# Input loads sent out in turns behind the squares of the feed-forward, and a reordered head, in a fused sparse-attention and feed-forward kernel

## The chip, the cores and the metric

The kernel runs on one NeuronCore of a Trainium2 chip. The metric is the device time of one execution, in microseconds (us); the lower, the better. The engines are TensorE (PE; its weight loads are shown as PEld), VectorE (DVE), ScalarE (ACT), GpSimd (POOL) and SyncE (SP). Each works through its own queue in order, and semaphores tie them together. POOL and SP also issue transfers (DMAs).

## What is computed

Batch 8, 8 heads, 576 tokens, head size 64; model width 512, hidden width 2048.

```python
scores = scale * np.matmul(q, k.transpose(0, 1, 3, 2))
rel = pos[:, None] - pos[None, :]
mask_local   = (rel >= 0) & (rel < 32)
mask_strided = (rel >= 0) & (pos[None, :] % 32 == pos[:, None] % 32)
# heads 0-3 use mask_local, heads 4-7 mask_strided
attn = softmax(where(mask, scores, -1e9))
x = (attn @ v) as [batch * 576, 512]           # 4608 tokens
h = x @ w_in                                   # 512 -> 2048
g = s * relu(h)**2 + b
out = g @ w_out                                # 2048 -> 512
```

Inputs and outputs are fp32; on the chip the kernel works in fp16 and sums in fp32. The loads that POOL issues convert from fp32 to fp16 on the way.

## The kernel before

**Attention.** A batch is cut into four pairs of heads, m = 0 and 1 local, m = 2 and 3 strided (`pair_steps`). The local heads are cut into 6 bands of 96 queries, so that a band needs 128 keys: its own 96 and the 32 before; `rows_before` copies those 32 rows of v to the partitions ahead. The strided heads are cut into residue groups of 72 tokens. For each pair, q and k have to be brought with the head size onto the partitions. In early batches PE does that (transposes at L429 and L437); in later ones a DMA transpose on SP does: `k_dma` (L480: local from batch `KB_DMA` = 4, strided from 3) and `q_dma` (L502: local from `QB_DMA` = 6, strided from `QS_DMA` = 3), after which `q_spread` copies q into a block-diagonal tile. PE then makes scores (L557), ACT takes the exponential (L575), DVE applies the mask (L583), PE multiplies by v (L614), and DVE divides by the row sums (L629, L640). The result x is transposed into `xT` by PE (L662) or by DMA; strided pairs of batches 4 to 6 take the way over `x_dram`, a store and a transposing load (`x_out`, `x_in`; `XS_DMA` = 4).

**Feed-forward.** It runs over 9 blocks T of 512 tokens. First product: 16 tiles of 128 hidden units, each of four 128x128x512 matmuls (L907). ACT takes the relu (L934) and DVE or ACT squares two tiles at a time into `gT` (L944, L942). One such pair of tiles is a pair of squares. Second product: L965 for blocks 0 to 2; from block 3 on L875, a seven-product form. `keep_running` (L1201) puts matmuls without use into the first microseconds, where PE has no data yet.

**Loads.** `load_qk`, `load_vl` and `load_vs` issue a batch's loads on POOL: local q and k (`ql`, `kl`, in four pieces of one head each where they go to a DMA transpose), strided q and k (`qs`, `ks`), v of the local heads (`v_loc`, the bands) and v of the strided heads (`v_str`, in early batches over `vs`). In `fetch_qk` a one-element copy into `gate` on POOL (L1036) waits for the transposes of the batch before, and then the whole batch is issued at once. Batch 0's v of local heads comes by SP into `vl_stage`, as fp32, in four loads, and POOL casts it. w_in comes in three pieces (512, 512 and 1024 columns), w_out in four. `second` issues batch 1 and w_out after batch 0 and w_in.

**Order.** The order on all engines is fixed when the kernel is built, by a planner (`Plan`). It keeps an estimated clock `plan.t` along PE's work. A `Step` is a piece of PE work with its needs; a post is work for another engine, given out by `flush` once its needs are met on the estimated clock, to the engine that would end first. `LAT` is what is added to an engine's end before its result counts as there ("D", "X" and "Y" stand for SP's transposes, stores of x and loads of x); `landing` does the same for loads. PE takes attention steps while they lag behind their due share (`due`), feed-forward steps otherwise. Only the order comes out of this: on the chip semaphores decide when each instruction starts.

Of the kernel before, what the change touches and what calls it, by code (L numbers as in the profile page):

```python
# [9 lines left out]
FP16 = mybir.dt.float16  # L10
# [5 lines left out]
class Plan:  # L16
# [7 lines left out]
    LAT = {"A": 70.0, "V": 70.0, "P": 70.0, "D": 12000.0, "X": 7000.0, "Y": 12000.0}  # L24
# [4 lines left out]
    def __init__(self):  # L29
        self.t = 0.0  # L30
        self.done = {}
        self.pend = []
        self.free = {"A": 0.0, "V": 0.0, "P": 7000.0, "D": 0.0, "X": 0.0, "Y": 0.0}
        self.banks = {}
# [82 lines left out]
class Step:  # L117
    def __init__(self, fn, ns, needs=(), group=None, keys=(), posts=(), after=None):
        self.fn, self.ns, self.needs, self.group = fn, ns, needs, group
        self.keys, self.posts, self.after = keys, posts, after  # L120
# [3 lines left out]
def kernel(  # L124
# [11 lines left out]
    nc = tc.nc  # L136
# [20 lines left out]
    for p in range(SQ):  # L157
        for c in range(SQ):
# [30 lines left out]
               for i, n in enumerate((512, 512, 1024))]  # L189
# [21 lines left out]
    def x_free(b):  # L211
# [22 lines left out]
    vl_stage = w_out_sb.rearrange("p f m -> p (f m)").bitcast(FP32)[:, 0:NL].rearrange(  # L234
        "p (h t d) -> p h t d", h=4, d=D)
# [34 lines left out]
    for tl in p_bufs[False]:  # L270
        nc.vector.memset(tl[:, 16 * SQ:], 0.0)

# [40 lines left out]
    def load_vl(b):  # L313
        vl = v_loc[b % NV]
        for h in range(4):
            nc.gpsimd.dma_start(out=vl[LPAD:128, h, :, 0:D], in_=v_band(b, h))  # L316
# [8 lines left out]
    def load_w_in():  # L325
        wv = moe_w_in.rearrange("(c p) f -> p c f", p=128)
        for i, at in enumerate((0, 512, 1024)):
            nc.gpsimd.dma_start(out=w_in_sb[i], in_=wv[:, :, at:at + w_in_sb[i].shape[2]])
# [26 lines left out]
    def cast_v(b, loc, mm, key):  # L355
        nt, np_, dst = (LT, 128, v_loc) if loc else (ST, SQ, v_str)

        def g(eng):
            src = vl_stage if loc else loaded[b, "vs"].rearrange(
                "p (h t d) -> p h t d", h=4, d=D)  # L360
            for h in range(2 * mm, 2 * mm + 2):
                copy_on(eng, out=dst[b % NV][0:np_, h, :, 0:D], in_=src[:, h])
        n = nt * D
        plan.post([key], {"P": 1000.0} if loc else {"A": 2 * (170 + 0.83 * n), "V": 540.0,
                                                           **({"P": 1500.0} if b == 0 else {})}, g,
                  [("cast", b, mm) if loc else ("in", "vs", b, mm)])
        if loc:
            rows_before(b, mm, ("cast", b, mm))

    def rows_before(b, mm, key):  # L370

        hs = slice(2 * mm, 2 * mm + 2)
        vl = v_loc[b % NV]
        src = vl_stage[:, :, :, 0:D] if b == 0 else vl[:, :, :, 0:D]

        def g(eng):
            copy_on(eng, out=vl[0:LPAD, hs, 1:LT, 0:D], in_=src[128 - LPAD:128, hs, 0:LT - 1])
        plan.post([key], {"P": 800.0} if b == 0 else {"A": 700.0, "V": 350.0}, g, [("in", "vl", b, mm)])
# [30 lines left out]
    def pair_steps(b, m):  # L409
# [10 lines left out]
        def trans(name, j, group):  # L420
            alone = loc and b < HEAD_T

            def f():
                if j == 0:
                    st["p" + name] = bank(group).bitcast(FP16)[:, 0:S]
                if alone:
                    for e in range(2):
# [12 lines left out]
            s = Step(f, 70 if alone else 35, needs=[("in", name + sfx, b, mm)],  # L440
                     group=group if j == 0 else None)
            if j == nt - 1:
# [35 lines left out]
        x_by_dma = b >= 2 if loc else XS_DMA <= b < B - 1  # L478
# [418 lines left out]
    def ff1(T, ft, ct, group, cts=(0, 1, 2, 3), early=False):  # L897
        tok0 = T * PS
        def f():
            if ft == 0 and ct == cts[0]:  # L900
                gts[T] = gp.tile([128, NFT, PS], FP16, tag="gT", name="gT")
            if ct == cts[0]:
                gts["h", T, ft] = bank(group)
            at = tok0 % (NX * S)
            n = min(PS, NX * S - at)
            for lo, hi in ((0, n), (n, PS))[:1 + (n < PS)]:
                nc.tensor.matmul(  # L907
                    out=gts["h", T, ft][:, lo:hi],
                    lhsT=w_in_sb[min(ft // 4, 2)][:, ct].rearrange(
                        "p (c x l) -> p c l x", x=128, l=4)[:, max(ft // 4 - 2, 0), ft % 4],  # L910
                    rhs=xT[ct][:, (at + lo) % (NX * S):(at + lo) % (NX * S) + hi - lo],
                    start=(ct == cts[0] and lo == 0), stop=(ct == cts[-1] and hi == PS))
# [109 lines left out]
    def landing(cost):  # L1022

        nonlocal ring
        ring = max(ring, plan.t + 2000.0) + cost

        return ring + (6000.0 if plan.t > 60000.0 else 600.0)
# [4 lines left out]
    def fetch_qk(b):  # L1032
# [6 lines left out]
        for name in ("q", "k"):  # L1039
            if b >= (QB_DMA if name == "q" else KB_DMA):  # L1040
                arrive(both(name + "l", b), landing(4600))
                continue
            if b < HEAD_T:
                arrive(both(name + "l", b), landing(1500))
                continue
            plan.done["raw", name, b] = landing(1700 if b > 1 else 1450)
            for mm in range(2):
                pair_post(b, name, mm, ("raw", name, b))
        for name in ("qs", "ks"):
            arrive(both(name, b), landing(2000 if b > 1 else 1750))  # L1050
# [12 lines left out]
    def early_v(b):  # L1063
# [3 lines left out]
        plan.done["raw", "v", False, b] = landing(1800)  # L1067
# [3 lines left out]
    gate = const.tile([64, 4], FP16)  # L1071

    def after_landing(i, src):
# [3 lines left out]
    load_qk(0)  # L1077
    early_v(0)
    plan.free["P"] = 7100.0
    plan.free["V"] = 6500.0  # L1080
    AT = {"ql0": 5700.0, "kl0": 6800.0, "ql1": 7900.0, "kl1": 8900.0, "qs": 10100.0,
          "ks": 11600.0, "vs": 13600.0, "vl0": 7100.0, "vl1": 14700.0}
# [6 lines left out]
    stage_v(range(2, 4))  # L1089
# [3 lines left out]
    def weights_in(eng):  # L1093
# [4 lines left out]
        ring = 15300.0  # L1098
        for keys, cost in ([0], 2700), ([1], 2500), ([2, 3], 5000):
            arrive([("w_in", c) for c in keys], landing(cost))  # L1100

    for mm, at in (0, AT["vl0"]), (1, AT["vl1"]):
        plan.done["raw", "v", True, 0, mm] = at
        cast_v(0, True, mm, ("raw", "v", True, 0, mm))
# [7 lines left out]
    def second(eng):  # L1112
# [3 lines left out]
        plan.done["raw", "vl", 1] = landing(3200)  # L1116
# [5 lines left out]
    plan.post(both("vl", 0) + both("vs", 0) + [("w",)], {"P": 14000.0}, second, [("free",)])  # L1122
# [12 lines left out]
    for b in range(B):  # L1135
        for m in range(4):
            steps, last_av = pair_steps(b, m)
            att.append(steps)
            if b + 2 < B:

                if m == 0:
# [4 lines left out]
                        {"P": 2900.0 + (2200.0 if b + 2 >= QB_DMA else 0.0)},  # L1146
                        lambda eng, b=b: fetch_qk(b + 2), [("fetch", b + 2)])
                last_av.after = when_all("av", b, lambda b=b: plan.post(
                    [("fetch", b + 2)] + both("vs", b), {"P": 3600.0}, lambda eng: fetch_v(b + 2),
                    [("fetch_v", b + 2)]))  # L1150

    f1, f2 = [], []
    for T in range(NBLK):
# [26 lines left out]
        for ts in range(4):  # L1180

            parts = 2 if T == NBLK - 1 and ts == 3 else 1
            for part in range(parts):
                gr = Group("f2", F2B)
                for ft in range(NFT):
                    f2.append(ff2(T, ts, ft, gr, part, parts))
                    f2[-1].pos = T + 0.25 + (ts + (part + ft / NFT) / parts) / 4
    def keep_running(until):

        ghz = 1.2 if plan.t < 6000 else 2.4  # L1190
# [26 lines left out]
    while i2 < len(f2) or any(at_i[p] < len(att[p]) for p in range(len(att))):  # L1217
# [5 lines left out]
        active = [p for p in range(first, min(first + 4, len(att))) if at_i[p] < len(att[p])]  # L1223
        for p in active:
# [67 lines left out]
```

## Time and profile before

| | |
|---|---|
| time, median of 3 runs | 305.44 us (305.16 to 306.75) |
| the profiled execution: its time | 306.2 us |
| the profiled execution: its span, first to last instruction | 304.4 us |
| PE / PEld busy | 296.4 / 205.8 us |
| DVE / ACT / POOL busy | 216.6 / 183.9 / 99.3 us |
| granted PE clock | 1.00 throughout |
| read from HBM / written | 36.86 / 10.32 MB |
| packets of the DMAs | 100826, of them 80907 under 512 B |

The page cuts the span into 40 slices of 7.6 us; the mean busy share of the 16 DMA engines is at nine tenths or more in nearly all of the first 200 us, and PE is at 8 or 9 tenths throughout. In the profile's rows an entry such as `out<-in xcount` counts instructions with the same tiles; "[... <-X]" names what ended the idle time before a row. The duration of a matmul in the records [...]379 ns for 512 columns that start 216 ns apart. So counts are multiplied by the distance of starts here, and not by that mean. An issue time on POOL or SP is not the time of the transfer; a transfer's "us to landing" is given apart.

### The profile page before, as it was taken

What the parts mean: (1) busy time and instruction counts of PE and PEld (TensorE: products, weight loads), DVE (VectorE), ACT (ScalarE), POOL (GpSimd) and SP (SyncE); (2) the same over time, 40 slices, a digit from 0 to 9 for tenths busy, and PEclk for the clock granted to TensorE, in tenths of its full rate; (3) what the DMA queues carried; (4) which work ended last, traced back from release to release, by engine and by line L of the source; (5) the groups of instructions that cost most, each with busy time, mean ns of one, the idle gap of its engine ahead of it and who ended that gap; (6) DMA issues with size and microseconds to landing.
All of it is one profiled execution on the core that took longest, in us unless ns stands there. A gap on an engine that the chain in (4) does not pass through costs nothing.

```text
span 304.4 us, 6800 instructions
## 1 busy us (share of the span) xinstructions
PE 296.4 (97%) x2674; PEld 205.8 (68%) x2674; DVE 216.6 (71%) x474; ACT 183.9 (60%) x330; POOL 99.3 (33%) x146
## 2 busy tenths in 40 slices
PE   8998999999999999999999999999999999999995
PEld 3764655666555568767567776778888666766784
DVE  6665897698966688737997698777765366737563
ACT  2966963898747677478585946695725445445300
POOL 8771753930961095029502961200000000000000
PEclk9999999999999999999999999999999999999999
DMA  8999999999999699999999999944010200300123
GB/s 136 183 201 202 137 213 190 179 198 149 83 160 165 98 100 149 132 186 147 142 153 172 142 160 159 155 105 131 14 37 34 72 34 0 106 0 2 69 82 126
DMA packets 100826, 37.29 MB, mean 122 GB/s; under 512 B 80907, under 2 KB 97803, under 8 KB 100795
## 3 DMA queue, kind: packets, MB, share of 16 engines
q0 software_dynamic: 57232, 18.08, 60.1%
q1 hardware_dynamic: 43562, 18.78, 33.3%
q8 instruction: 21, 0.34, 0.5%
q14 instruction: 11, 0.08, 0.1%
HBM read 36.86 MB, written 10.32 MB: 155 GB/s over the span
## 4 chain that ended last, share of the span: by engine, by line
PE 83%; DMA 8%; DVE 3%; POOL 3%; issue 1%; ACT 1%; POOLq 0%
PE ps_f L907 36%; PE ps_f L875 20%; PE ps_f L965 12%; DMA kl<-in_k_dram 5%; PE ps_s L557 3%; PE ps_a L614 3%; DMA vs<-in_v_dram 2%; PE ps_s L875 2%; DMA xT<-x_dram 1%; PE ps_t L875 1%; PE ps_s L965 1%; PE ps_t L614 1%; PE ps_t L662 1%; PE ps_t L437 1%; PE ps_f L437 1%
## 5 line engine op out<-in xcount | busy, mean ns | idle before, releaser
L907 PE MATMUL ps_f<-xT,w_in_sb 128*128 128x512 f16 (+4 forms) x696 | 148.1, 340 | 0.0
L934 ACT ACTIVATE u<-ps_f 128x512 f16<-128x512 f32 x137 | 80.8, 595 | 72.6 <-PE ps_f L907 69.9
L907 PEld LDWEIGHTS <-w_in_sb 128*128 128x128 f16 x704 | 71.7, 113 | 33.1 <-DMA w_in_sb<-in_moe_w_in_dram 0.5
L875 PEld LDWEIGHTS <-gT 128*128 128x128 f16 x512 | 49.0, 98 | 12.5 <-issue 0.4
L965 PE MATMUL ps_f<-w_out_sb,gT 128*128 128x512 f16 x176 | 47.6, 379 | 0.0
L875 PE MATMUL ps_f<-w_out_sb,gT 128*128 128x256 f16 x312 | 44.2, 273 | 0.3 <-DVE o L806 0.3
L944 DVE TENSOR_TENSOR gT<-u 128x1024 f16<-128x1024 f16 x46 | 32.1, 697 | 15.1 <-ACT u L934 14.4
L942 ACT ACTIVATE gT<-u 128x1024 f16<-128x1024 f16 x26 | 27.5, 1057 | 0.7
L640 DVE TENSOR_TENSOR x_nat<-ps_a,rec 72x256 f16<-72x256 f32 (+1 forms) x55 | 25.3, 459 | 0.9
L316 POOL DMA_DIRECT2D v_loc<-in_v_dram x28 | 20.7, 759 | 14.3 <-DMA w_in_sb<-in_moe_w_in_dram 6.0
L965 PEld LDWEIGHTS <-gT 128*128 128x128 f16 x192 | 17.0, 98 | 11.1
L575 ACT ACTIVATE p_str<-ps_s 72x432 f16<-72x432 f32 (+1 forms) x45 | 20.1, 481 | 4.7 <-PE ps_s L557 4.6
L575 ACT ACTIVATE p_loc<-ps_s 128x384 f16<-128x384 f32 x46 | 20.8, 494 | 2.2 <-PE ps_s L557 1.8
L614 PEld LDWEIGHTS <-p_str 72*128 72x128 f16 x256 | 15.3, 98 | 7.3 <-issue 0.4
L747 DVE TENSOR_TENSOR gT<-gT 128x1024 f16<-128x1024 f16 x28 | 18.5, 683 | 1.4 <-ACT gT L942 1.3
L875 PE MATMUL ps_f<-w_mix,gT 128*128 128x256 f16 x144 | 19.3, 273 | 0.0
L875 PEld LDWEIGHTS <-S 128*128 128x128 f16 x160 | 15.5, 98 | 3.7
L629 DVE RECIPROCAL rec<-ps_a 72x4 f32<-72x4 f32 (+1 forms) x55 | 9.7, 177 | 11.2 <-PE ps_a L614 11.0
L321 POOL DMA_DIRECT2D v_str<-in_v_dram x16 | 13.0, 816 | 9.6 <-PE ps_f L907 5.6
L583 DVE TENSOR_TENSOR p_loc<-p_loc,masks 128x1152 f16<-128x1152 f16 x14 | 10.5, 750 | 7.6 <-ACT p_loc L575 7.4
L875 PE MATMUL ps_f<-w_mix,S 128*128 128x256 f16 x96 | 13.4, 273 | 0.0
L976 DVE SCALAR_TENSOR_TENSOR o<-ps_f,s_sb,bcs 128x512 f32<-128x512 f32 x11 | 8.2, 749 | 6.4 <-PE ps_f L965 6.2
(162 smaller groups left out, 413.2 us busy)
## 6 DMA issues: line engine op xcount, KB each, us to landing
out_dram<-o SPq DMA_DIRECT2D x34, 256.0 KB, 3.4
w_out_sb<-in_moe_w_out_dram POOLq DMA_DIRECT2D x4, 512.0 KB, 9.4
v_loc<-in_v_dram POOLq DMA_DIRECT2D x28, 72.0 KB, 8.5
qs<-in_q_dram POOLq DMA_DIRECT2D x6, 288.0 KB, 6.6
ks<-in_k_dram POOLq DMA_DIRECT2D x6, 288.0 KB, 8.0
ql<-in_q_dram POOLq DMA_DIRECT2D x5, 288.0 KB, 9.7
kl<-in_k_dram POOLq DMA_DIRECT2D x16, 72.0 KB, 3.8
v_str<-in_v_dram POOLq DMA_DIRECT2D x16, 72.0 KB, 9.9
```

Of the source, the lines that this page charges most:

```text
L316: nc.gpsimd.dma_start(out=vl[LPAD:128, h, :, 0:D], in_=v_band(b, h))
L321: nc.gpsimd.dma_start(out=vs[:, h, :, 0:D], in_=v[b, 4 + h].rearrange("(p j) d -> p j d", j=ST))
L575: nc.scalar.activation(out=st["pw", g][0:nk, 0:2 * n * nq], in_=st["s", g][0:nk, 0:2 * n * nq], func=AF.Exp, scale=scale)
L614: nc.tensor.matmul(out=st["a"][:, j % per, :], lhsT=st["pw", g][0:nk, i * nq:i * nq + WIDE], rhs=vt[0:nk, 2 * mm + e, j, :])
L640: nc.vector.tensor_tensor(out=st["x"][:, j0:j0 + per, 64 * e:64 * e + 64], in0=st["pa", e, j][0:nq, 0:per, 0:D], in1=st["rec", e, j][0:nq, ...
L747: nc.vector.tensor_tensor(out=at(out), in0=at(x), in1=at(y), op=op)
L875: nc.tensor.matmul(out=gts[name, T, t][:, 0] if halves else gts[name, T][:, t], lhsT=lhs(k, t), rhs=rhs(k), start=fresh and k == 0 and (ha ...
L907: nc.tensor.matmul(out=gts["h", T, ft][:, lo:hi], lhsT=w_in_sb[min(ft // 4, 2)][:, ct].rearrange("p (c x l) -> p c l x", x=128, l=4)[:, ma ...
L934: nc.scalar.activation(out=u, in_=gts["h", T, ft], func=AF.Relu)
L942: nc.scalar.activation(out=g, in_=u, func=AF.Square)
L944: nc.vector.tensor_tensor(out=g, in0=u, in1=u, op=ALU.mult)
L965: nc.tensor.matmul(out=gts[id_], lhsT=gts[T][:, ft, ts * 128:(ts + 1) * 128], rhs=w_out_sb[:, ft, cols], start=(ft == 0), stop=(ft == NFT ...
```

## The change

Seven things change together.

- **Turns.** From batch 4 (`SPREAD`) on, the loads of a batch are no longer issued at once. `spread_qk` and `spread_v` hand each load singly to `in_turn`. It groups them by `PER` = 3; the first of each group does a one-element copy from `gT` on POOL, which waits for a given pair of squares of the running block. The copies that wait for the transposes of k now stand ahead of the `ks` load only.
- **Planner.** `LAT` of D goes from 12000 to 7000 ns, of X from 7000 to 5500, of Y from 12000 to 5500; a queue "Z" without cost is added for posts that only hand out others. `landing` adds 4000 ns instead of 6000 after 60 us. Loads in turns count as landed 5000 ns after their issue.
- **Head, v of batch 0.** Only heads 0 and 1 come by SP through `vl_stage`; heads 2 and 3 come by one load on POOL, right into `v_loc`, ahead of `vs`.
- **v of batch 1** (the second band v) comes in one load rather than four.
- **w_in** comes in four pieces of 512 columns.
- **x of the last batch**: the strided pairs of batch 7 also take the way over `x_dram`.
- **Start.** The planner's clock starts at 1850 ns, the expected arrivals (`AT`) change, batch 0's transposes keep together once begun (`sticky`), and small parts of the `p_str` tiles are zeroed at the start.

```diff
-    LAT = {"A": 70.0, "V": 70.0, "P": 70.0, "D": 12000.0, "X": 7000.0, "Y": 12000.0}
+    LAT = {"A": 70.0, "V": 70.0, "P": 70.0, "D": 7000.0, "X": 5500.0, "Y": 5500.0, "Z": 0.0}
...
-               for i, n in enumerate((512, 512, 1024))]
+               for i, n in enumerate((512, 512, 512, 512))]
...
+        nc.vector.memset(tl[:, 0:12 * SQ].rearrange("p (g x) -> p g x", g=2)[:, 1, 0:56], 0.0)
+        nc.vector.memset(tl[:, 12 * SQ:12 * SQ + 56], 0.0)
...
     def load_vl(b):
         vl = v_loc[b % NV]
+        if b < 2:
+            nc.gpsimd.dma_start(
+                out=vl.rearrange("p h t d -> p (h t) d")[LPAD:128, :, 0:D],
+                in_=v.rearrange("b h (t p) d -> b p (h t) d", p=LQ)[b, :, 0:4 * LT])
+            return
...
-        x_by_dma = b >= 2 if loc else XS_DMA <= b < B - 1
+        x_by_dma = b >= 2 if loc else XS_DMA <= b
...
+    SPREAD, PER, LATE = 4, 3, 5000.0
+    turn = [0, 0]
+
+    def in_turn(fns, needs=()):
+
+        if turn[0] <= i1 // 8:
+            turn[0], turn[1] = i1 // 8 + 1, 0
+        for fn, keys in fns:
+            T, at = turn[0] // 8, turn[0] % 8
+            key = ("g", T, ff_order(T)[2 * at]) if T < NBLK else None
+
+            def go(eng, fn=fn, key=key, first=turn[1] == 0):
+                if first and key:
+                    nc.gpsimd.tensor_copy(out=gate[0:1, 0:1], in_=gts[key[1]][0:1, key[2], 0:1])
+                fn()
+            plan.post(list(needs) + [key] * (key is not None), {"P": 760.0}, go, keys, LATE)
+            turn[1] += 1
+            if turn[1] == PER:
+                turn[0], turn[1] = turn[0] + 1, 0
...
+            def load(name=name, src=src, ts=ts):
+                for mm in range(2) if name == "k" else ():
+                    if (b - 1, "kTs", mm) in loaded:
+                        nc.gpsimd.tensor_copy(out=gate[0:1, 2 + mm:3 + mm],
+                                              in_=loaded[b - 1, "kTs", mm][0:1, 0, 0:1])
+                if name == "q" and b == QS_DMA + 1:
+                    nc.gpsimd.memset(ts[64:SR], 0.0)
+                load_s(ts, src, b)
+            fns.append((load, both(name + "s", b)))
+        in_turn(fns)
...
+    nc.gpsimd.dma_start(
+        out=v_loc[0].rearrange("p h t d -> p (h t) d")[LPAD:128, 2 * LT:4 * LT, 0:D],
+        in_=v.rearrange("b h (t p) d -> b p (h t) d", p=LQ)[0, :, 2 * LT:4 * LT])
     early_v(0)
...
-    stage_v(range(2, 4))
...
-                        lambda eng, b=b: fetch_qk(b + 2), [("fetch", b + 2)])
+                        lambda eng, b=b: (spread_qk if b + 2 >= SPREAD else fetch_qk)(b + 2),
+                        [("fetch", b + 2)])
...
+    plan.t = 1850.0
...
+        active.sort(key=lambda p: not att[p][at_i[p]].sticky)
```

## The prediction

> **What bounds the kernel now.** I read the page's busy times first, then what TensorE (PE) waited for, then the order of its instructions at its longest waits, then POOL's queue.
>
> ```profile
> span 304.4 us, 6800 instructions
> PE 296.4 (97%) x2674; PEld 205.8 (68%) x2674; DVE 216.6 (71%) x474; ACT 183.9 (60%) x330; POOL 99.3 (33%) x146
> ```
>
> PE is busy for 97% of the span. The waits of PE say how much of the rest another engine could give back:
>
> ```profile
> PE ps_t L429 <- DMA ql<-in_q_dram: 1.4, 1, 1.4
> PE ps_s L1201 <- DVE w_mix L257: 1.1, 1, 1.1
> PE ps_t L429 <- DMA kl<-in_k_dram: 0.6, 1, 0.6
> PE ps_s L557 <- ACT kT_loc L338: 0.4, 1, 0.4
> PE ps_s L907 <- DMA w_in_sb<-in_moe_w_in_dram: 0.4, 1, 0.4
> PE ps_f L875 <- DVE o L806: 0.3, 1, 0.3
> PE ps_a L614 <- DVE x_nat L640: 0.2, 1, 0.2
> ```
>
> The columns are the total, the number of times and the longest, in us. Only the last two (0.5 us) fall after 33 us. From there on PE has work without a break until it ends at 301.2 us, and 3.2 us for the last output follow. So a gain can only come from the first 33 us or from less PE work; any new wait of PE after that is paid in full. In the head, PE's timeline:
>
> ```profile
> 23.00 4.05 PE L907 MATMUL ps_f<-xT,w_in_sb 128*128 128x512 f16 x18
> 28.49 0.45 PE L429 MATMUL ps_t<-ident,ql 96*64 96x96 f16 x12 [1.44 <-DMA ql<-in_q_dram]
> 28.77 0.42 PE L429 MATMUL ps_f<-ident,ql 96*64 96x96 f16 x12
> 29.12 1.49 PE L907 MATMUL ps_f<-xT,w_in_sb 128*128 128x512 f16 x6
> 31.23 0.45 PE L429 MATMUL ps_t<-ident,kl 96*64 96x96 f16 x12 [0.62 <-DMA kl<-in_k_dram]
> ```
>
> PE stands twice for batch 1: q lands at 28.5 us, k at 31.2. Whatever was lost or saved before 26.9 us is swallowed by the first of these waits. POOL's queue at the same time:
>
> ```profile
> 22.06 0.75 POOL L316 DMA_DIRECT2D v_loc<-in_v_dram  x1 [1.96 <-DMA w_in_sb<-in_moe_w_in_dram]
> 26.89 0.72 POOL L316 DMA_DIRECT2D v_loc<-in_v_dram  x1 [4.08 <-DMA w_in_sb<-in_moe_w_in_dram]
> 28.73 0.73 POOL L316 DMA_DIRECT2D v_loc<-in_v_dram  x1 [1.11 <-DMA ql<-in_q_dram]
> 31.47 0.72 POOL L316 DMA_DIRECT2D v_loc<-in_v_dram  x1 [2.01 <-DMA kl<-in_k_dram]
> ```
>
> Each load waits for the eighth load before it on this queue, so four v loads for batch 1 hold back all behind them. What the DMAs move falls from about 200 GB/s (17 to 30 us) to 51 at 32 us.
>
> [...]kT transposes land 2.9 us after issue (median), but qTl, issued at 150.8 and 180.5 us behind outstanding v loads, 8.6 to 9.3, and kT_alt at 119.9 us 9.9. [...]Dense runs of L907 here start 216 ns apart.
>
> **The change part by part.** The order of the built instructions, not only the diff, is used.
>
> Batch 7's strided x goes through DRAM: 16 PE transposes (80 to 64 of 72 columns) go. They start 32.5 ns apart in the trace (four in 0.13 us): **−0.5 us**. Added are two stores and two DMA transposes on SP. PE ends batch 7's attention some 16 us of its own work before the last block needs x; store, landing (3.4 as an output's), transpose (1.2) and its landing (2.7 to 4.8) make 8 to 10 and fit, and the DMA share there is below 0.25. With less room it could cost up to 2 us: kept for the range.
>
> Head. 32 matmuls of L907 still precede batch 1's q, but ten, not six, now precede its k: 4 × 0.216 = 0.86 us of work in place of a gap of 0.78 us (start to start, less the work): **−0.8**. The q wait itself: two of the four SP loads of batch 0's v (144 KB each) become one POOL load that writes half the bytes, 144 KB less ahead of q at about 200 GB/s: 0.7 us, between 0 (if packets, not bytes, count) and 1.0 (the dip at 13 to 16 us also goes): I take **−0.6**. w_in goes in four pieces: one POOL issue more (0.76), hidden because q lands after w_in anyway; the third piece is asked for only after q, at 29 us. One v load of batch 1 in place of four saves 3 × 0.73 us of POOL and lets w_out start some 2 us sooner; PE did not wait for w_out, so nothing. At worst its first head lands with the last, later by what three issues took (2.2 us), and PE asks for v 7 us after k: nothing. POOL loses a CAST of 1.2 us and two copies (1.16) ahead of q, DVE halves a memset of 1.34 and gains four small ones (about 0.06 each), PE's warm-up matmuls fall from 13 to 8 (0.43 us each, while it waits for the first q): all before 26.9 us, nothing. The planner's shorter latencies only change the order.
>
> Spread loads, batches 4 to 7. Before, batch 4's loads issue from 76.2 to 92.3 us and its scores start near 108. After, five or six gates copy one element of gT, then three loads follow each. In PE's order the first gate stands 20 us later, at 95.8 us of the old clock (its pair of squares ends 93.8; evicting and squaring take about 2). POOL issues 15 loads × 0.745 = 11.2 us, a memset of 1.8 and gates of some 2.5: again about 16 us. So the burst is hardly thinner, it is **later**. No PE work is saved. What becomes late is SP's transposes and q_spread. Behind a waiting gate stand POOL's other loads and no PE work directly; behind a late load on SP stand x and output transfers.
>
> The longest chain is strided k (load_s, then k_dma). From the first gate to the end of ks's issue I count 10.6 us for batch 4 (nine loads, memset, five gate copies with gaps of 0.45), 8.7 for 5, 11.3 for 6 (SP also has an x transpose of 1.3 ahead), 12.1 for 7. Then the load lands (288 KB rows: 5.2 to 8.3), SP issues (1.3), the transpose lands (2.9 quiet, 5.3 under loads as qT's). Sum: 20.0 to 25.5, 18.1 to 23.6, 22.0 to 27.5, 21.5 to 27.0. PE's own work from that gate to the first score that reads it: 20.6, 22.2, 23.4, 25.4. So the wait is 0 to 4.9, 0 to 1.4, 0 to 4.1, 0 to 1.6. Local q of batch 6 and 7 (qTl at 9 us) ends within 0.5 of its need. Since gates also hold later loads back, I take the low ends: **+0.2**, at most about 12.
>
> Sum: −0.5 − 0.8 − 0.6 + 0.2 = **−1.7 us**. The profiled execution took 306.2 us (span 304.4 and 1.8 around it), 0.8 above the median of 305.44. So 304.5 against that execution, and **303.7** against the median.
>
> **Rivals.** *Late k, slower*: the load and the transpose meet the same traffic as before, 8.3 and 5 us. For is that the burst keeps its 16 us and that transposes of 9 us occur amid loads; against, that the kT transposes all landed in 2.9 to 4.4. Priced at half of the upper waits (2.4 + 0.7 + 2 + 0.8 = 5.9) less the 1.9 gained: 309.4; at a quarter, 306.5. It decides for batch 4 from load plus transpose over 8.7 us (20.6 − 10.6 − 1.3); above 1.9 us over all batches it makes a loss. *Paid back, no change*: q of batch 1 lands at 28.5 as before and the chains cost 1 us: −1.3 + 1.0 gives 305.1. *The spread does nothing*: POOL is so far behind its gates that they never hold; then order and head alone count, 303.5; for it, issue time almost fills the gates' pace.
>
> **How the numbers follow.** A measurement of this kernel can tell about 0.5% (1.5 us) from no change: below 303.9 is faster, above 307.0 slower. Faster (head gain kept, chains in time, the third rival with it) 0.49; within 0.5% 0.26; slower by late k 0.25. The likeliest is 303.7. Its own range is 301.9 (q a further microsecond earlier, other head gaps gone) to 304.6 (the q wait kept). The range over the cases, 301.9 to 308.8, leaves out some 0.07 below and 0.13 above.
>
> **What would show it.** Right: PE's wait for kl gone and that for ql at or under 1.4 us; 64 transposes of x; no PE wait over 0.5 us on kT, kT_alt or qD; kT landing near 3 us. Wrong: PE (or its weight load) waiting at scores of batches 4 to 7 near 116, 146, 180 or 211 us, with kT landings over 4.5 us or ks over 6; or q of batch 1 landing later than 28.5.

## The result: an eighth slower, and the profile after

The changed kernel takes 347.81 us (median of 4 runs, 343.12 to 351.9); the kernel before, on the same chip, took 306.09 (305.16 to 306.75). The ratio is 1.125 (95% interval 1.116 to 1.135); it is taken from the two faster runs (343.12 and 345.58 us) alone, because the other two, the profiled one among them, lie over 1.5% above the fastest and ran at a lower granted clock (0.946 and 0.951 against 0.960). I had said 303.7, in a range of 301.9 to 308.8. The profiled execution is the longest of the four, so its waits are rather long. In the kernel of the first experiment below, profiled at 340.93 us, those for k and for `x_nat` stand again: kT_alt 9.2, kT_loc 4.7, kT 1.6 and x_nat 3.9 us.

The page of the changed kernel, busy times and granted clock (tenths of full speed in 40 slices of 8.75 us):

```profile
span 350.1 us, 6790 instructions
PE 310.0 (89%) x2658; PEld 211.7 (60%) x2658; DVE 209.3 (60%) x475; ACT 192.7 (55%) x334; POOL 100.3 (29%) x161
PEclk9899987999999969999699978999699999999999
```

PE has 16 matmuls fewer, yet is busy for 13.6 us more (310.0 against 296.4), and it stands for 40.1 us instead of 8.0. The two differences, 13.6 and 32.1, are the whole 45.7 us between the spans. The dips in the last row show why fewer matmuls take longer: part of them run at a lower clock (0.50 from 124 to 128 us, for one). What PE stands for is in its waits (total, times, longest, in us):

```profile
PE ps_s L565 <- DMA kT_alt<-kl: 9.0, 3, 5.8
PE ps_f L622 <- POOL v_str L345: 6.6, 1, 6.6
PE ps_a L622 <- DVE x_nat L648: 6.6, 2, 4.3
PE ps_s L565 <- DMA kT_loc<-kl: 5.8, 1, 5.8
PE ps_s L565 <- DMA kT<-ks: 3.6, 1, 3.6
```

Of these five only the third stood in the list of before, with 0.2 us. They are of three kinds: k that comes late (18.4 us), v that POOL casts late (6.6), and x that DVE divides late (6.6).

**Late k.** POOL's queue at the loads of batches 4 and 6, then SP's queue and PE at batch 6's first local scores:

```profile
102.59 0.18 POOL L1093 COPY gate<-gT 1x1 f16<-1x1 f16 x1 [21.33 <-DVE gT L951]
...
182.98 0.34 POOL L1093 COPY gate<-gT 1x1 f16<-1x1 f16 x1 [26.55 <-ACT gT L949]
...
188.99 1.45 POOL L1108 DMA_DIRECT2D kl<-in_k_dram  x2 [0.20 <-issue]
```

```profile
191.51 4.07 SPq L516 DMA_TRANSPOSE qTl<-ql  x2
195.69 3.73 SPq L497 DMA_TRANSPOSE kT_loc<-kl  x2
```

```profile
199.97 1.58 PE L883 MATMUL ps_f<-w_mix,gT 128*128 128x256 f16 x13
207.33 0.82 PE L565 MATMUL ps_s<-qD_loc,kT_loc 128*128 128x192 f16 x4 [5.77 <-DMA kT_loc<-kl]
207.94 0.85 PE L883 MATMUL ps_f<-w_mix,gT 128*128 128x256 f16 x3
```

POOL stands 27 us at a gate, and only then asks for batch 6. From the gate's copy on it is 7.5 us to the end of kl's last issue, 5.3 more until SP gets to kl's transposes (behind two of q), and 11.6 more until they land: together 24.3 us. PE was there after 18.6. The last row is the second cost: three matmuls of 256 columns take 0.85 us, where three of them took 0.49 at 199.64 us, before the wait.

**Late v.** The loads of v stand behind gates too. DVE works in order: it stands at the copies of v's 32 rows (`rows_before`), and the divisions that PE waits for come behind them. DVE's timeline:

```profile
119.39 0.32 DVE L345 COPY v_loc<-v_loc 32x640 f16<-32x640 f16 x1 [4.47 <-DMA v_loc<-in_v_dram]
119.74 0.42 DVE L648 TENSOR_TENSOR x_nat<-ps_a,rec 72x256 f16<-72x256 f32 x1
```

**The cast of batch 1.** The change also lets POOL copy batch 1's strided v into `v_str`, where only batch 0's could go before; the list of the change above leaves this out. The planner did give that copy to POOL, where it stands behind loads that wait for w_out's, and PE waits for it. POOL, then PE:

```profile
45.28 0.73 POOL L323 DMA_DIRECT2D v_loc<-in_v_dram  x1 [1.98 <-DMA w_out_sb<-in_moe_w_out_dram]
47.77 0.73 POOL L323 DMA_DIRECT2D v_loc<-in_v_dram  x1 [1.76 <-DMA w_out_sb<-in_moe_w_out_dram]
49.27 0.73 POOL L313 DMA_DIRECT2D vs<-in_v_dram  x1 [0.77 <-DMA ql<-in_q_dram]
50.05 1.17 POOL L345 COPY v_str<-vs 72x512 f16<-72x512 f16 x2
```

```profile
50.71 0.38 PE L622 MATMUL ps_f<-v_str,p_str 72*128 72x65 f16 x4 [6.58 <-POOL v_str L345]
```

**The head.** PE, where it stood for q and k of batch 1 before, and POOL's load that waits for q to land:

```profile
28.46 0.45 PE L436 MATMUL ps_t<-ident,ql 96*64 96x96 f16 x12
28.74 0.42 PE L436 MATMUL ps_f<-ident,ql 96*64 96x96 f16 x12
29.09 2.35 PE L915 MATMUL ps_f<-xT,w_in_sb 128*128 128x512 f16 x10
31.37 0.45 PE L436 MATMUL ps_t<-ident,kl 96*64 96x96 f16 x12
```

```profile
27.83 0.56 POOL L313 DMA_DIRECT2D vs<-in_v_dram  x1 [0.68 <-DMA ql<-in_q_dram]
```

Both waits (1.4 and 0.6 us) are gone, with ten matmuls where six stood. But that is not yet a gain of 1.4 us. q did land 0.9 us sooner (the load behind it goes out at 27.83 us, before at 28.73), yet PE transposes it at 28.46 us, before at 28.49: PE itself came 1.4 us later. At k, PE starts 0.14 us later than before, with 0.86 us more of its work done; so 0.7 us is what the head has gained here.

### The profile page after: what moved, and what is told of

The parts are those of the page before. It is cut to its first block, busy times and chain, and to the rows that moved or that the text cites. A ratio compares the mean times of both kernels' runs of the same rounds, so it can differ in the third digit from the quotient of the medians.

```text
span 350.1 us, 6790 instructions
## 1 busy us (share of the span) xinstructions
PE 310.0 (89%) x2658; PEld 211.7 (60%) x2658; DVE 209.3 (60%) x475; ACT 192.7 (55%) x334; POOL 100.3 (29%) x161
## 4 chain that ended last, share of the span: by engine, by line
PE 64%; DMA 25%; POOL 3%; SPq 2%; issue 2%; DVE 2%; ACT 1%; POOLq 0%
PE ps_f L915 27%; PE ps_f L883 14%; PE ps_f L972 8%; DMA kT_alt<-kl 6%; DMA kT<-ks 5%; DMA ql<-in_q_dram 4%; PE ps_s L565 4%; DMA v_loc<-in_v_dram 3%; DMA kT_loc<-kl 3%; DMA xT<-x_dram 3%; PE ps_a L622 2%; DMA kl<-in_k_dram 2%; PE ps_s L883 1%; SPq L516 1%; PE ps_t L883 1%
## 5 line engine op out<-in xcount | busy, mean ns | idle before, releaser
L883 PEld LDWEIGHTS <-gT 128*128 128x128 f16 x512 | 51.1, 101 | 13.3
L972 PE MATMUL ps_f<-w_out_sb,gT 128*128 128x512 f16 x176 | 53.1, 406 | 0.1
L883 PE MATMUL ps_f<-w_out_sb,gT 128*128 128x256 f16 x312 | 47.1, 283 | 0.0
L949 ACT ACTIVATE gT<-u 128x1024 f16<-128x1024 f16 x33 | 34.9, 1058 | 1.2
L951 DVE TENSOR_TENSOR gT<-u 128x1024 f16<-128x1024 f16 x39 | 26.6, 683 | 14.7 <-ACT u L941 14.1
L1093 POOL COPY gate<-gT 1x1 f16<-1x1 f16 x22 | 6.8, 308 | 93.2 <-DVE gT L951 58.2
L583 ACT ACTIVATE p_loc<-ps_s 128x384 f16<-128x384 f32 x46 | 21.3, 487 | 17.2 <-PE ps_s L565 16.6
L972 PEld LDWEIGHTS <-gT 128*128 128x128 f16 x192 | 18.1, 103 | 11.9 <-issue 1.6
L755 DVE TENSOR_TENSOR gT<-gT 128x1024 f16<-128x1024 f16 x28 | 18.6, 679 | 4.5 <-ACT gT L949 4.4
L883 PE MATMUL ps_f<-w_mix,gT 128*128 128x256 f16 x144 | 20.2, 286 | 0.0
L565 PE MATMUL ps_s<-qD_loc,kT_loc 128*128 128x192 f16 x68 | 13.1, 280 | 5.8 <-DMA kT_loc<-kl 5.8
L883 PEld LDWEIGHTS <-S 128*128 128x128 f16 x160 | 15.6, 98 | 4.1
L622 PE MATMUL ps_a<-v_str,p_str 72*128 72x65 f16 x140 | 10.7, 197 | 6.9 <-DVE x_nat L648 6.6
L345 ACT COPY xT<-ps_t 128x576 f16<-128x576 f16 x7 | 4.5, 639 | 22.0 <-PE ps_t L670 19.5
L345 DVE COPY v_loc<-v_loc 32x640 f16<-32x640 f16 x10 | 3.2, 324 | 20.5 <-DMA v_loc<-in_v_dram 20.3
```

Of the source, the lines that this page charges most:

```text
L565: nc.tensor.matmul(out=st["s", g][0:nk, c:c + 2 * nq], lhsT=(st["k"][:, i * nq:i * nq + nk] if loc else st["k"][:, i, 0:SQ]), rhs=st["q"][ ...
L583: nc.scalar.activation(out=st["pw", g][0:nk, 0:2 * n * nq], in_=st["s", g][0:nk, 0:2 * n * nq], func=AF.Exp, scale=scale)
L622: nc.tensor.matmul(out=st["a"][:, j % per, :], lhsT=st["pw", g][0:nk, i * nq:i * nq + WIDE], rhs=vt[0:nk, 2 * mm + e, j, :])
L755: nc.vector.tensor_tensor(out=at(out), in0=at(x), in1=at(y), op=op)
L883: nc.tensor.matmul(out=gts[name, T, t][:, 0] if halves else gts[name, T][:, t], lhsT=lhs(k, t), rhs=rhs(k), start=fresh and k == 0 and (ha ...
L949: nc.scalar.activation(out=g, in_=u, func=AF.Square)
```

## The experiments

Each median is compared with that of the kernel before, measured beside it on the same chip (305.9 to 306.7 us). Of the fourteen kernels, eleven build on the first, which takes the cast back, and two on the kernel before.

### The cast of batch 1, taken off POOL

```diff
-                                                           **({"P": 1250.0} if b < 2 else {})}, g,
+                                                           **({"P": 1250.0} if b == 0 else {})}, g,
```

> The changed kernel, but the copies of batch 1's strided v into v_str may no longer go to POOL (in cast_v POOL stays a choice for batch 0 only). Theory (three causes that add: a copy stuck on POOL behind loads, data in turns that lands later than the order assumes, and a slow TensorE clock after long waits): TensorE's wait of 6.6 us at 44 us goes with the slow clock after it (0.68 from 50 to 60 us, some 3 us), so about 10 us less: 336 to 340 against 347.8. Rival (that copy is the whole loss): 303 to 308. Rival (the wait is hidden, because the data of the next batches are late anyway): 345 to 349.

340.65 us (ratio 1.112, 1.106 to 1.117), just above my 336 to 340. The wait of 6.6 us is gone. Against the two runs that the ratio of the changed kernel is taken from (344.4 us on average), the cast is worth 3.7 us; the two intervals overlap a little, so its size is uncertain. The other 34 us are in the main late k and v. POOL's gates of batch 4 at its q and k, in this kernel:

```profile
95.44 0.18 POOL L1093 COPY gate<-gT 1x1 f16<-1x1 f16 x1 [32.40 <-DVE gT L951]
...
97.78 0.18 POOL L1093 COPY gate<-gT 1x1 f16<-1x1 f16 x1
...
103.92 0.18 POOL L1093 COPY gate<-gT 1x1 f16<-1x1 f16 x1
```

Only the first gate waits. The later ones are open when POOL comes to them, and so it is with q and k of batches 5 to 7 (first gates 20.7, 21.2 and 13.6 us, the others at once); only at v's gates POOL stands again, up to 7.6 us. So the turns do not thin the burst; they make it late. "Cast back" below means this edit.

### Turns undone, with the short and the long latencies

Cast back, and `SPREAD` = 99, so that all batches are asked for at once:

```diff
-    SPREAD, PER, LATE = 4, 3, 5000.0
+    SPREAD, PER, LATE = 99, 3, 5000.0
```

> As e1, and without turns: SPREAD is 99, so batches 4 to 7 are loaded at once as before; head and short planner latencies (D 7000) stay. Theory (the turns are the main loss, since they put loads some 20 us later): the long waits for kT_loc, kT_alt and v rows go, 304 to 312. Rival (the short latencies are the main loss: PE asks for transposes after 8 us that take 9 to 12): 325 to 340, with PE waiting for kT_alt and kT again.

312.23 us (1.019, 1.012 to 1.026), at the upper end of the theory. With these latencies the turns account for 28.4 us.

The other way round, cast back, turns kept, and the planner's latencies as before:

```diff
-    LAT = {"A": 70.0, "V": 70.0, "P": 70.0, "D": 7000.0, "X": 5500.0, "Y": 5500.0, "Z": 0.0}
+    LAT = {"A": 70.0, "V": 70.0, "P": 70.0, "D": 12000.0, "X": 7000.0, "Y": 12000.0, "Z": 0.0}
...
-        return ring + (4000.0 if plan.t > 60000.0 else 600.0)
+        return ring + (6000.0 if plan.t > 60000.0 else 600.0)
...
-    SPREAD, PER, LATE = 4, 3, 5000.0
+    SPREAD, PER, LATE = 4, 3, 12000.0
```

> As e1 with the turns, but the planner reckons with long latencies: D 12000, X 7000, Y 12000, landing 6000 as before, and 12000 for loads in turns in place of 5000. Theory (a load that waits for squares comes too late whatever the order, since the squares themselves wait for attention): PE's waits for DMA shrink to under 5 us in all, but PE has no other work in those places and the time stays at 335 to 350. Rival (only the estimates were wrong): 304 to 312.

339.37 us (1.108, 1.105 to 1.112): longer estimates do not help while the gates hold the loads. k is gone from the list of PE's waits. In its place stand x on its way over `x_dram` and what DVE makes for the feed-forward; the two longest:

```profile
PE ps_f L915 <- DMA xT<-x_dram: 5.6, 2, 4.1
PE ps_f L883 <- DVE w_mix L777: 3.4, 1, 3.4
```

One reading, not tried by itself: with long estimates the attention is put off until its data are there, and then the feed-forward lacks its x.

Last, both undone (`SPREAD` = 99 and the old `LAT` and `landing`), so that the head, w_in in four, v in one load and batch 7's x are what is left:

> The reordered head, w_in in four pieces, the one v load of batch 1 and x of batch 7 over DRAM, without turns and with the long latencies; the copies of batch 1's strided v not on POOL. Theory (the head gains what the prediction says): 303 to 304.5, with PE's wait for kl gone and that for ql under 1.4 us. Rival (the head does not matter or costs): 305 to 308.

307.9 us (1.004, 1.001 to 1.007). My 303 to 304.5 missed; the head comes back below.

### The short latencies alone, in the kernel before

```diff
-    LAT = {"A": 70.0, "V": 70.0, "P": 70.0, "D": 12000.0, "X": 7000.0, "Y": 12000.0}
+    LAT = {"A": 70.0, "V": 70.0, "P": 70.0, "D": 7000.0, "X": 5500.0, "Y": 5500.0}
...
-        return ring + (6000.0 if plan.t > 60000.0 else 600.0)
+        return ring + (4000.0 if plan.t > 60000.0 else 600.0)
```

> The kernel before, with only the planner's assumed latencies of the change: 7.0 us for a store and 5.5 us for a transpose where 12 and 7 (or 12) stood, and 4 us instead of 6 for a load. Loads, turns and head are those of before. Theory: two kernels that differ in these numbers alone and have the new head stood at 312.2 and 307.9, so the numbers alone cost about 4 us: 309 to 312, with PE waits of 1 to 2 us on kT and kT_alt at scores of batches 4 to 6. Rival A: they cost only where the new head has used up the slack: 306 to 307.5, no PE wait over 0.5 us after 35 us. Rival B: the loss between those two kernels was the cold clock at their start and not the numbers: also 306 to 307.5, but then the kernel with the kept-warm head must gain more than 4 us.

314.84 us (1.025, 1.019 to 1.031): 8.9 us, twice what I expected, from numbers that change nothing but the order. Its longest wait of PE:

```profile
PE ps_s L557 <- DMA kT_loc<-kl: 3.9, 1, 3.9
```

The planner now thinks that kT_loc is there 7 us after SP's issue and puts its scores too early. (In the expectation the names are mixed up: 7.0 us is for SP's transposes, 5.5 for the stores and loads of x.)

### Turns without their wait

Cast back, pieces handed out singly, but no piece waits for squares:

```diff
-            key = ("g", T, ff_order(T)[2 * at]) if T < NBLK else None
+            key = None
```

> The change with the cast of batch 1 back on DVE or ACT (340.7 us when it ran) and the turns left in place, but without their wait: no load waits for a pair of squares, the pieces go out when their buffers are free. Theory: the 28 us that the turns cost come from POOL standing at the first gate of a batch (from about 75 to 95.4 us for batch 4), which makes every load of the batch some 20 us later; without it the loads start near 76 and 104 us: 310 to 316. Rival A: it is the split into pieces and the 5 us that the planner assumes for them, not the waiting: 330 to 340. Rival B: waits of loads for the eighth load before them take the gates' place: 318 to 328, with POOL waiting for DMA between loads.

327.0 us (1.056, 1.047 to 1.066). The wait accounts for 13.6 us here, not for all 28: neither the theory nor rival A had it. The figure lies in the range of rival B, and POOL does wait for DMAs between these loads (eight times from 60 us on, up to 1.8 us). To tell rival B from the estimates, the same once more with the long latencies of the diff further up:

> The change with the cast of batch 1 back on DVE or ACT, pieces sent out without any wait for squares, and the planner's assumed latencies of the kernel before (store 12, transpose 7 or 12, pieces landing 12 us after issue instead of 5). The same without the wait but with the short latencies stood at 327.0; with the wait and the long latencies at 339.4. Theory: what was left of the loss without the wait (327.0 against 312.2 with all loads of a batch asked for at once) is the planner's 5 us for pieces that in fact land 8 to 12 us after issue, so that it places scores too early: 308 to 313, no PE wait over 1.5 us after 45 us. Rival: sending the pieces out the moment that they are asked for brings them among the loads of the batch before, and that costs whatever the planner assumes: 320 to 330.

307.45 us (1.004, 1.002 to 1.007), just under the theory's 308 to 313 and level with the loads asked for at once (307.9). POOL still waits for DMAs between its loads, up to 1.7 us, so rival B is not what cost the 20 us. The four kernels with turns make a table (medians, us; "short" includes the 5 us, "long" the 12 us that a load in turns is taken to need):

| | short latencies | long latencies |
|---|---|---|
| pieces wait for squares | 340.65 | 339.37 |
| pieces do not wait | 327.0 | 307.45 |

Either fault alone costs 20 us (short latencies) or 32 us (wait); with both, 33. They do not add; why was not tried further. Which of the short numbers makes up the 20 us was not tried either: with all loads at once, where the 5 us plays no part, they cost 4.3 us (312.23 less 307.9). PE's longest waits without the gates' wait, with short latencies, then with long:

```profile
PE ps_a L622 <- DVE x_nat L648: 3.0, 1, 3.0
PE ps_f L915 <- ACT u L941: 2.1, 2, 1.9
PE ps_s L565 <- ACT p_loc L583: 2.1, 1, 2.1
PE ps_s L565 <- DVE qD_loc L345: 1.4, 1, 1.4
```

```profile
PE ps_s L1286 <- DVE w_mix L257: 1.1, 1, 1.1
PE ps_t L436 <- DMA ql<-in_q_dram: 0.9, 1, 0.9
PE ps_f L622 <- DVE p_loc L591: 0.6, 1, 0.6
```

With the long latencies nothing over 1.1 us is left. Cutting the loads into pieces costs nothing then.

### The first gate a pair earlier; turns for v alone

```diff
-        if turn[0] <= i1 // 8:
-            turn[0], turn[1] = i1 // 8 + 1, 0
+        if turn[0] < i1 // 8:
+            turn[0], turn[1] = i1 // 8, 0
```

> As the change with the cast of batch 1 back on DVE or ACT (340.7 us when it ran), but the turns begin one pair of squares earlier: behind the pair that is under way when the loads are asked for, not behind the next. Pace and number per turn stay. Theory: what costs is the place of the first gate alone, since the later turns of a batch were already open when POOL came to them; a pair is some 10 to 20 us of PE's time, so the loads come that much sooner and most of the waits go: 311 to 322, with later gates that hold POOL for some us each. Rival: the pace of the turns costs, and one pair at the start gives back only its share: 332 to 338.

336.27 us (1.095, 1.089 to 1.102), the rival's figure; but that does not bear the rival out. Batch 4's first gate opened at 93.43 us instead of 95.44, those of batches 5, 6 and 7 opened 0.7, 6.5 and 2.0 us sooner, where I had counted on 10 to 20: the edit hardly moved what it was to move, and says little.

The second is cast back, with `fetch_qk` in place of `spread_qk` for all batches, given to POOL as before:

```diff
-                        {"Z": 0.0} if calm else {"P": 2900.0},
-                        lambda eng, b=b: (spread_qk if b + 2 >= SPREAD else fetch_qk)(b + 2),
+                        {"P": 2900.0},
+                        lambda eng, b=b: fetch_qk(b + 2),
```

> The change with the cast of batch 1 back on DVE or ACT (340.7 us when it ran), with turns for v alone: q and k of batches 4 to 7 are asked for at once, as before. Theory: the loss lies in k and q, whose loads are followed by a transpose and then scores: 313 to 320, with no PE wait over 2 us on kT, kT_loc or kT_alt; v has no transpose behind it and is needed 7 us after k. Rival A: v that comes late holds DVE in its copies (v_loc to v_loc), and with it everything behind on DVE, so most of the loss stays: 328 to 338, with PE waiting for x_nat or p_loc from DVE. Rival B: POOL standing at the gates of v's turns holds back q and k of the batch after: also 328 or more, but with PE waiting for kT.

312.4 us (1.019, 1.010 to 1.028), just under the theory's 313 to 320 and the same as with all loads at once and these latencies (312.23). The loss lies in the turns of q and k. v in turns by itself costs nothing: DVE's copies then wait 3.4 us for v in all, where they waited 20.3 in the changed kernel and 21.3 with the cast back.

### PE kept at work through two waits

The slow clock looked like a cost of its own. With the cast back, the granted clock is 0.66 in the three stretches of 10 us in which waits of 3.9, 4.7 and 6.4 us end (110 to 120, 190 to 200, 230 to 240 us), and 1.00 in one in which PE stood for 2.4 us in all (140 to 150). So cast back once more, with matmuls whose results are overwritten, ahead of the scores that waited longest:

```diff
+                if loc and b in (6, 7) and i == 0 and ("fill", b) not in loaded:
+                    loaded["fill", b] = True
+                    for _ in range(16 if b == 6 else 24):
+                        nc.tensor.matmul(
+                            out=st["s", g][:, 0:512], lhsT=ones16,
+                            rhs=ones16[:, None, :].to_broadcast([128, 4, 128]),
+                            start=True, stop=True)
```

> The change with the cast of batch 1 back on DVE or ACT (340.7 us when it ran), with work added and none taken away: 16 more matmuls of 512 columns (3.5 us at the fast clock) ahead of the first local score of batch 6, where PE waited 4.7 us for kT_loc, and 24 (5.2 us) ahead of that of batch 7, where it waited 6.4 us for kT_alt. Their results are written over. Theory: after each of these waits PE ran at half clock for some 7 us (granted clock 0.66 in 190 to 200 and 230 to 240 us), which costs 3.4 us each; kept at work through the waits it stays at the full clock, so the kernel gets faster by 5 to 7 us although it does more: 333 to 336, with a clock of 1.00 in those stretches. Rival A: the lower clock is not brought about by the standing still: 340 to 342. Rival B: the waits shrink once the clock is fine, so that the added matmuls are paid for: 338 to 345.

342.96 us (1.123, 1.113 to 1.133): no gain; my theory fell. PE's timeline (the edit moves L565 to L572 and L883 to L890) and three stretches of 10 us (the column before the last two is the clock):

```profile
187.68 3.62 PE L562 MATMUL ps_s<-w_mix 128*128 128x512 f16 x16
193.14 0.50 PE L572 MATMUL ps_s<-qD_loc,kT_loc 128*128 128x192 f16 x4 [1.85 <-DMA kT_loc<-kl]
...
228.78 5.34 PE L562 MATMUL ps_s<-w_mix 128*128 128x512 f16 x24
235.83 0.50 PE L572 MATMUL ps_s<-qD_loc,kT_alt 128*128 128x192 f16 x4 [1.70 <-DMA kT_alt<-kl]
```

```profile
190.00:200.00 10.00, 5.73 (x52) 3.95 (x51) 5.90 (x13) 8.59 (x14) 1.79 (x3) 1.00 1.71 132
200.00:210.00 10.00, 7.89 (x61) 4.99 (x61) 3.85 (x11) 5.16 (x11) 0.00 (x0) 0.83 0.49 110
230.00:240.00 10.00, 7.76 (x53) 4.57 (x50) 2.05 (x5) 4.87 (x9) 0.80 (x1) 1.00 1.82 117
```

The clock stayed up in the two filled stretches (0.66 in both without the fillers), which rules out rival A. But PE got to k's scores no sooner (193.14 against 192.59 us, 235.83 against 233.19), and after the first the time won went into the next wait: PE then stood 3.3 us for xT, up to 202.1 us, where it had stood 0.9. The clock fell behind that wait instead (0.83 from 200 to 210 us, where it had been 1.00), so part of the half clock was moved and not taken away. The figure is rival B's. As far as these two waits show, data sets the pace here, and the half clock is paid out of time that PE would stand anyway.

### The head

What ate the head's 2 us? The first loss is in PE's first scores, first of the kernel before, then of the new head alone. Starts are in the first column:

```profile
9.03 0.25 PE L557 MATMUL ps_s<-qD_loc,kT_loc 128*128 128x192 f16 x1
9.11 0.25 PE L554 MATMUL ps_s<-w_mix,ident 128*128 128x192 f16 x1
```

```profile
8.64 0.37 PE L562 MATMUL ps_s<-w_mix,ident 128*128 128x192 f16 x1
8.80 0.37 PE L565 MATMUL ps_s<-qD_loc,kT_loc 128*128 128x192 f16 x1
```

Starts are 83 ns apart before, 160 ns after. The slow stretch goes from 8.35 to 12 us, so at most 1.8 us are lost, half of it. PE had stood for 0.5, 0.8 and 0.4 us between 4.5 and 8 us, with 8 warm-up matmuls instead of 13 ahead. For all that, this head is about 0.9 us ahead at k of batch 1: its transposes start at 31.14 us, before at 31.23, with four matmuls of 512 columns (0.86 us) more done. A new wait then takes as much away, at 41.7 us:

```profile
PE ps_f L622 <- DVE p_loc L591: 1.0, 1, 1.0
```

It stands in the other kernels with the new head and the long latencies too (0.5 to 1.5 us) and in the kernel before not at all; its cause was not followed. The experiments went after the clock: the new head with the warm-up restored (the fillers behind q are counted at the fast clock, so they get about twice the columns):

```diff
-    plan.t = 1850.0
+    plan.t = 950.0
...
-        ghz = 1.2 if plan.t < 6400 else 2.4
+        ghz = 1.2 if plan.t < 5200 else 2.4
```

> The new head without turns and with the old latencies (307.9 us when it ran), and the warm-up of PE made whole again: two more warm-up matmuls of 512 columns ahead of the first q, and the fillers behind that q counted at the fast clock, so that they last twice as long. Theory: the new head gained about 2 us at q and k of batch 1 and lost 1.6 to 1.9 us at the scores from 8.35 to 12 us, which started 160 ns apart instead of 83 because PE had stood for 1.7 us between 4.5 and 8 us; with PE kept at work they run at 83 ns: 305.5 to 306.5, a clock of 1.00 in the first 20 us, and 0 to 1 us below the kernel before. Rival: the slow clock at the start is caught up before 27 us by other work waiting for data, so nothing changes: 307.5 to 308.3. Second rival: the longer fillers hold up q's and k's transposes more than the clock gives: 308 to 309.

307.83 us (1.005, 1.001 to 1.009), the first rival's figure and not the theory's. The scores ran 83 ns apart, but the half clock came elsewhere, 20.6 to 24 us, after a stretch of small waits:

```profile
20.00:22.00 2.00, 1.97 (x17) 1.18 (x16) 1.75 (x7) 1.13 (x4) 0.40 (x1) 0.64 1.24 207
22.00:24.00 2.00, 2.00 (x9) 0.83 (x8) 0.00 (x0) 0.48 (x1) 0.15 (x1) 0.50 1.25 210
```

Nine more matmuls without use fill that stretch too: the one below ahead of each of the eight groups of batch 0's strided values, and one of 512 columns ahead of the first square (not shown).

```diff
+                    if b == 0 and not loc:
+                        nc.tensor.matmul(
+                            out=bank(group)[:, 0:384], lhsT=ones16,
+                            rhs=ones16[:, None, :].to_broadcast([128, 3, 128]),
+                            start=True, stop=True)
```

> The new head with its warm-up kept at work (307.8 us when it ran), and nine more matmuls whose results are written over: one of 384 columns ahead of each of the eight groups of batch 0's strided values, one of 512 ahead of the first square, together 1.5 us of PE at the fast clock, in a stretch (16 to 21 us) where PE stood for about 1.5 us and after which it ran at half clock from 20.6 to 24 us. Theory: what the new head gains at q and k of batch 1 (2 us) is lost to that stretch of half clock; with PE kept at work there [...]the kernel comes out 1 to 2 us lower: 305.5 to 307, level with the kernel before or up to 1 us below it. Rival A: the added matmuls cost what the clock gives back: 307.3 to 308.5. Rival B: the half clock comes all the same, somewhere else in the first 30 us: 308 to 309.5.

307.39 us (1.005, 1.003 to 1.006), the figure of rival A: the clock was 1.00 throughout, but the added matmuls cost what it gave back. PE's last matmuls, in the chain that ended last (start, length), of the kernel before and of this one:

```profile
300.37 0.89 PE ps_f L875 x8
```

```profile
300.10 0.89 PE ps_f L888 x8
```

PE is done 0.27 us sooner, with 1.5 us of added work. But the span (304.9 against 304.4) ends 3.9 us after it instead of 3.1. Two kernels seek the reason in batch 7's x. In the first it is back on PE in the filled head (the diff); in the second it alone goes into the kernel before, by the same line the other way round:

```diff
-        x_by_dma = b >= 2 if loc else XS_DMA <= b
+        x_by_dma = b >= 2 if loc else XS_DMA <= b < B - 1
```

> The filled new head (307.4 us when it ran) with batch 7's strided x transposed on PE again, as before. Theory: the kernels with the new head end 3.9 us or more after PE's last matmul where the kernel before ended 3.1 after it, and batch 7's x over DRAM is what they share: with it undone the end comes 0.8 sooner and PE has 0.5 us more to do: 306.5 to 307.2, 3.1 us between PE's end and the span's. Rival: the later end has another cause, and the 16 transposes only add their 0.5 us: 307.5 to 308.3, with 3.8 us or more at the end.

307.35 us (1.005, 1.003 to 1.007), between the theory and the rival: the end comes 3.3 us after PE (305.1 less 301.8), about as the theory said, but PE ends 0.8 us later, 0.5 of it for the 16 transposes. The time stays where it was: what the one gives the other takes.

> The kernel before with batch 7's strided x through DRAM and nothing else changed. Theory: PE has 0.5 us less to do, but the span ends 3.9 us after PE instead of 3.1: level, 305.8 to 306.7. Rival A: the gain of 0.5 us that I predicted for this part, with the end as before: 305.3 to 305.8. Rival B: x comes late for the last block and PE waits up to 2 us: 307 to 308.

307.34 us (1.004, 1.001 to 1.006), slower than the kernel before by itself. The end comes 3.8 us after PE (306.0 less 302.2), and PE ends 1.0 us later, not 0.5 sooner, with a new wait of 0.8 us for DVE's `Va` near 239 us and two for w_out before 51 us, 0.8 together; it is rival B's figure, but PE does not wait for x. In both pairs the kernel with this part ends 0.6 to 0.7 us later after PE. All traces agree: the end comes 3.1 to 3.4 us after PE in the three kernels without this part and 3.8 to 4.7 in the thirteen with it. Why stays open. None of these kernels beats the one before.

## Why the prediction was wrong

**Right.** The q and k waits of batch 1 are gone, with ten matmuls ahead of k, and q landed 0.9 us sooner where I had said 0.6. The place of batch 4's first gate: I had said 95.8 us, it was 95.44 with the cast back. That the burst is hardly thinner but later: so it is; only the first gate held q and k. The rival *late k, slower* named the mechanism, though not its size.

**Wrong: "I take the low ends: +0.2".** This is the step that cost most: the turns cost 28.4 us. I let a load land in 5.2 to 8.3 us and a transpose in 2.9 to 5.3, and took the low figures although I had listed transposes of 9 us amid loads. In the changed kernel kT lands in 7.2 to 8.1 us, kT_loc in 7.9 to 11.6, kT_alt in 9.6, and strided k in 8.1 to 12.3; with the cast back the figures are much the same (kT_loc 6.9 to 11.0, strided k 8.0 to 12.3). The upper ends would have made 12 us, still short of the 18.4 that PE stood for k. Even the late-k rival halved its upper waits and came to 309.4.

**Wrong: strided k as the longest chain.** Of the 18.4 us of waits for k, 14.8 are for local k (kT_loc, kT_alt). PE asks for it first, and in batch 6 SP had two transposes of q to issue before it. The v of these batches I did not follow at all; it came back as DVE's copies, and PE's 6.6 us behind them.

**Wrong: batch by batch.** I set each gate against PE's clock of before. But the gates wait for squares, and squares wait behind PE's late scores: a wait in one batch puts off the loads of the next. With the cast back, batch 4's first gate opens 2.6 us sooner than PE of before would have opened it, counted by the first-product matmuls done; those of batches 5, 6 and 7 open 8, 14 and 23 us later.

**Wrong: "The planner's shorter latencies only change the order".** The order was worth 4.3 us with the new head, 8.9 in the kernel before and 20 with turns that do not wait (the 5 us for a load in turns included). On an estimate that is too short, PE is led to a step whose data are not there.

**Wrong: "POOL loses a CAST of 1.2 us and two copies (1.16) ahead of q", put at nothing.** The permission to copy `v_str` on POOL covered batch 1 too, and that copy came at 50 us. PE stood 6.6 us for it, and some 4 us of them show in the kernel's time.

**Wrong: the head's sum.** What came before 26.9 us was swallowed by the wait for q only as long as there was one. With q there sooner, PE came 1.4 us later, and the colder start (up to 1.8 us) counted: −0.6 was not there, and a new wait of 1.0 us for `p_loc` took away what −0.8 had given. The 16 transposes did come off PE's busy time (0.3 and 0.5 us in the two pairs that isolate them), but not off the kernel's: in both pairs its end came 0.6 to 0.7 us later after PE.

**Not in it: the clock.** In the changed kernel PE's busy time grew by 13.6 us, with the cast back by 9.0, though it has less to do; in part it ran at half speed (a granted clock of 0.50 from 124 to 128 and from 208 to 212 us in the changed kernel). Two filled waits gained nothing, so there it was no separate item; the other waits were not tried.

## What to carry to other kernels

To hold back a load, count from its issue to the last thing made of it, at the durations that the same transfers have amid the burst and not at their quiet ones (strided k's transposes landed in 2.9 to 4.4 us before, in 7.2 to 8.1 in the changed kernel), and for the tile that is asked for first. A gate that waits for the consumer's own progress turns slack into a loop: once PE is late, so is the next load. In this planner estimates that were too short cost 4 to 20 us; longer ones than those of the kernel before were not tried. And a wait that is taken away uncovers what it used to swallow.

## What the runs showed of the hardware

- In the new head alone, starts of matmuls doubled their distance (83 to 160 ns for 192 columns) after PE had stood for 1.7 us in three pieces within 3.5 us; with the warm-up restored, the granted clock was 0.50 from 22 to 24 us after waits of 0.4 us at most. Neither had a single wait over 0.8 us there; the waits ahead of the lower clock with the cast back were 3.9 to 6.4 us long. So one long gap is not the only way to the half clock.
- In one run the profile's clock seems to miss a slower stretch. From 9 to 10 us, with PE busy throughout, the kernel before has 13 matmuls at a granted clock of 1.00 and the changed kernel 9 at 0.50; with all loads at once there are 8, at 1.00. There the matmuls tell more than the clock does.
